# GpSimd makes the query tile with even columns first, and scores leave TensorE in natural column order

## The chip, the cores and the metric

One core of one Trainium2 chip runs the kernel. The metric is the device time of one execution in microseconds (us); a difference within 0.2% is not told from none. TensorE is PE in the profile (its weight loads PEld), VectorE is DVE, ScalarE is ACT, GpSimd is POOL, SyncE, which here only issues DMAs, is SP.

## The reference

Four batches, each with 3136 rows. A squared-ReLU attention with no softmax is followed by a feed-forward layer that has a three-tap convolution over the sequence and a sigmoid gate:

```python
scores = (1.0 / S) * np.matmul(z, z.transpose(0, 2, 1))   # S = 3136, z: (4, S, 64)
attn = np.maximum(scores, 0.0) ** 2
x = u * np.matmul(attn, v)                                # u, v: (4, S, 256)
h = np.maximum(x @ w_in, 0.0)                             # w_in: (256, 1024)
conv_out = sum(conv_w[k] * shifted(h, k - 1) for k in range(3))
out = (h * sigmoid(conv_out)) @ w_out                     # w_out: (1024, 256)
```

`z` meets itself, so the scores of a batch are a symmetric matrix.

## The kernel before

**Tiles and loops.** A batch's 3136 columns are six query blocks of 512 and a remainder of 64, and 25 key chunks of 128 (the last is half full). One pass of the main loop, a slot `k`, is one key chunk of one query block: 4 x 6 x 25 = 600 slots. In a slot PE makes the scores of a chunk four slots ahead (`scores`, two matmuls of 512 columns into the PSUM tile `s`) and adds the present chunk to the block's output (`attend`, L535). ACT takes the ReLU out of PSUM (`relu`, L490, tile `t`), DVE squares it (`square`, L504), ACT rounds the square to the high part `ah` (`split_hi`, L513), DVE subtracts to get the low part `al` (`split_lo`, a subtraction through the helper at L173). The feed-forward work of the block before is strewn between (`ffn_*`, L705 to L782). Which work stands in which slot is written out by hand: `at(slot, class, function)`; every engine takes its own instructions in that order. `manual_schedule` keeps it, and the pools only add waits.

**Two-part numbers.** Operands are `float32r` in a high and a low part: `zh`, `zl` for `z`. The rows 0 to 63 and 64 to 127 of `zh` and `zl` both hold `z`. The query tile `zq` of a block (two buffers, used in turn) holds `zh` in its lower 64 partitions and `zl` in its upper 64. Two DMAs per block, for all blocks but the first, copy it out of `zh` and `zl` (`query`, L225 and L226). The first block's is made by DVE out of the loaded `z` (`first_z`, L238 and L240). `query` for block `blk` stands eight slots ahead of the block's first slot (26 ahead for the last block of a batch).

**Reading in two streams.** `pairs` makes PE read the moving operand as columns 0, 256, 1, 257 and so on: two runs side by side. For `zq` that means that scores lie in PSUM with the two halves of the block interleaved. The consumers put it right: `split_hi` and `split_lo` read the tile through `unpair`, and so do `early_copy` (the last chunk's scores, made ahead) and the ReLU of the block's own chunks at L478. A key chunk on the diagonal reads only 256 columns, as 128 + 128.

**Reuse by symmetry.** A score tile below the diagonal isn't computed again. `part` (POOL, L434 for a whole tile; L431 and L432 for the first chunk on the diagonal) parts the ReLU tile `t` into its upper and lower 16 bits, into one of three buffers `pl`. `spill` (SP, L449) writes `pl` to DRAM, and `fetch` (SP, L457) brings it back transposed as `tp` in a later block. Where `t` came from interleaved scores (`k in mixed`), `part` also reorders: its source steps by two 4-byte numbers.

**The last chunk.** For blocks 2 to 23 the scores of chunk 24 are held as the tile `sh` and squared by DVE, which reads `sh` twice (`relu`, L482); DVE's subtraction for that chunk writes `ah` itself (64x512).

Of the kernel before, what the change touches and what calls it, by code (L numbers as in the profile page):

```python
# [8 lines left out]
F32 = mybir.dt.float32  # L9
F32R = mybir.dt.float32r  # L10
I32 = mybir.dt.int32
U16 = mybir.dt.uint16
U32 = mybir.dt.uint32
U64 = mybir.dt.uint64
AF = mybir.ActivationFunctionType
# [66 lines left out]
def kernel(  # L82
# [10 lines left out]
    nc = tc.nc  # L93
# [4 lines left out]
    P = 128  # L98
    NB = 512
# [11 lines left out]
    SC1 = 2.0**-12  # L111
# [36 lines left out]
    def at_slot(k):  # L148
        blk, i = divmod(k, NJ)
        return blk, *ent[blk // QB][blk % QB][i]  # L150
# [6 lines left out]
    zh = const.tile([P, NJ * P], F32R, name="zh")  # L157
    zl = const.tile([P, NJ * P], F32R, name="zl")
    zp = const.tile([P, P], F32R, name="zp")
# [12 lines left out]
    def sub(eng, out, a, b):  # L172
        eng.tensor_tensor(out=out, in0=a, in1=b.bitcast(F32), op=ALU.subtract)  # L173

    def copy(eng, out, a):
        (eng.copy if eng is nc.scalar else eng.tensor_copy)(out, a)  # L176


    def pairs(t):
        return t.rearrange("p (a i) -> p i a", a=2)  # L180

    def halves(t):
        return t.rearrange("p (a i) -> p a i", a=2)

    def unpair(t):
        return t.rearrange("p (i a) -> p a i", a=2)

    zst, vst, wst, wps = {}, {}, {}, {}
    LO, HI = slice(0, DQ), slice(DQ, P)
# [29 lines left out]
    zq = {}  # L219

    def query(blk):
        b, q = divmod(blk, QB)
        zq[blk] = t = mv.tile([P, NB], F32R, tag="zq", name="zq", bufs=2)
        c = slice(q * NB, (q + 1) * NB)
        nc.sync.dma_start(out=t[LO].bitcast(F32), in_=zh[LO, c].bitcast(F32))  # L225
        nc.sync.dma_start(out=t[HI].bitcast(F32), in_=zl[HI, c].bitcast(F32))  # L226

    def query_rem(b):
        zq["r"] = t = mv.tile([P, RQ], F32R, tag="zr", name="zr", bufs=1)
# [3 lines left out]
    def first_z():  # L233
        t, h = zst.pop(0), P
        v, a = nc.vector, nc.scalar
        zq[0] = x = mv.tile([P, NB], F32R, tag="zq", name="zq", bufs=2)
        copy(a, zh[:, :h], t[:, :h])
        copy(v, x, t)  # L238
        copy(a, zh[:, h:NB], t[:, h:])
        sub(v, x[HI], t[HI], x[HI])  # L240
        sub(v, zl[:, :h], t[:, :h], zh[:, :h])
        sub(v, zl[:, h:NB], t[:, h:], zh[:, h:NB])

# [104 lines left out]
    sc, ah, al, pav = {}, {}, {}, {}  # L348

    def own_cols(k):  # L350
        x = side(k)
        return slice(x * P, (x + 2) * P) if x else slice(0, NB)

    def odd(t):
        return t.rearrange("p (a b n) -> p a b n", a=2, b=2)[:, :, 1]
# [3 lines left out]
    def ring_score(blk):  # L359
        j = blk % QB * CB + CB - 1  # L360
        dg[blk] = p = ps.tile([P, 512], F32, tag="ph", name="ph", bufs=2)
        w = slice(j * P, (j + 1) * P)
        o, r = p[:, : NB // 2], odd(zq[blk]).rearrange("p a n -> p n a")
        nc.tensor.matmul(o, lhsT=zh[:, w], rhs=r, start=True, stop=False)
        nc.tensor.matmul(o, lhsT=zl[:, w], rhs=r, start=False, stop=True)

    def ring_relu(blk):
        p = dg[blk]
        dg[blk] = t = wk.tile([P, 1, 2 * NB], U16, tag="dg", name="dg", bufs=1)
        nc.scalar.activation(odd(t[:, 0].bitcast(F32)), unpair(p[:, : NB // 2]), AF.Relu, scale=SC1)  # L370

    def ring_part(blk):
        src = dg[blk][:, 0, 2 * P : 4 * P]
# [6 lines left out]
    def held(k):  # L380
        blk, j, _ = at_slot(k)
        return j == NJ - 1 and blk >= PK

    def scores(k):
        blk, j, tr = at_slot(k)
        if tr or held(k) or side(k) == CB - 1:
            return

        if k < K_O and k % 2:
            tag, n = ("ph", 2) if k < NJ else (f"o{k // 2 % 2}", 1)  # L390
        else:
            tag, n = "s", 2
        s = ps.tile([P, 512], F32, tag=tag, name="s", bufs=n)
        w, c = slice(j * P, (j + 1) * P), own_cols(k)
        r = pairs(zq[blk][:, c])
        nc.tensor.matmul(s[:, c], lhsT=zh[:, w], rhs=r, start=True, stop=False)  # L396
        nc.tensor.matmul(s[:, c], lhsT=zl[:, w], rhs=r, start=False, stop=True)  # L397
        sc[k] = s

    rl, pl, dq, dd, tp, mixed = {}, {}, {}, {}, {}, set()  # L400


    def rows_of(b, r):
# [10 lines left out]
    def part(k):  # L414
        blk, j, tr = at_slot(k)
        b, q = divmod(blk, QB)
        r, x = j // CB, side(k)
        if x is not None and x < CB - 1:
            src = rl[k][:, (x + 1) * P : (x + 2) * P if x else NB]
        elif x is None and not (tr or r < (Q0 if b == q == 0 else q + 1) or (r == QB and q >= RB)):  # L420
            src = rl[k]
        else:
            return
        n = src.shape[-1]
        pl[k] = wk.tile([P, 2, NB], U16, tag="pl", name="pl", bufs=3)[:, :, :n]
        src = src.bitcast(U16)
        if k in mixed:
            w = src.rearrange("p (i a h) -> p h a i", a=2, h=2)
            if x == 0:
                w = rl[k].bitcast(U16).rearrange("p (i a h) -> p h a i", a=2, h=2)  # L430
                nc.gpsimd.tensor_copy(pl[k][:, :, :P], w[:, :, 0, P:])  # L431
                nc.gpsimd.tensor_copy(pl[k][:, :, P:], w[:, :, 1])  # L432
            else:
                nc.gpsimd.tensor_copy(pl[k].rearrange("p h (a i) -> p h a i", a=2), w)  # L434
        else:
            nc.gpsimd.tensor_copy(pl[k], src.rearrange("p (n h) -> p h n", h=2))

    def spill(k):
        blk, j, _ = at_slot(k)
# [30 lines left out]
    def relu(k):  # L470
        x = side(k)
        if at_slot(k)[2] or x or held(k):
            if held(k):
                rl[k] = tp[k] = hs.pop(at_slot(k)[0])
            if x and x < CB - 1:
                rl[k] = tp[k]
                c = own_cols(k)
                nc.scalar.activation(halves(tp[k][:, c]), unpair(sc[k][:, c]), AF.Relu, scale=SC1)  # L478
            else:
                sc[k] = ps.tile([P, 512], F32, tag="s", name="s", bufs=2)  # L480
            if by_vector(k):
                nc.vector.scalar_tensor_tensor(  # L482
                    out=sc[k][:, :NB], in0=tp[k], scalar=SC1**-1, in1=tp[k], op0=ALU.mult, op1=ALU.mult
                )
            else:
                nc.scalar.activation(sc[k][:, :NB], tp[k], AF.Square, scale=SC1**-0.5)
            return
        mixed.add(k)
        rl[k] = wk.tile([P, NB], F32, tag="t", name="t", bufs=3)
        nc.scalar.activation(rl[k], sc[k][:, :NB], AF.Relu, scale=SC1)  # L490
        if act_squares(k):
            nc.scalar.activation(sc[k][:, :NB], rl[k], AF.Square, scale=SC1**-0.5)
# [13 lines left out]
    def split_hi(k):  # L506
        ah[k] = mv.tile([P, NB], F32R, tag="ah", name="ah", bufs=4)
        if k in tp:
            nc.scalar.activation(ah[k], tp.pop(k), AF.Square, scale=SC1**-0.5)  # L509
        elif k < DIR:  # L510
            nc.scalar.activation(ah[k], rl[k], AF.Square, scale=SC1**-0.5)
        else:
            nc.scalar.copy(halves(ah[k]), unpair(sc[k][:, :NB]))  # L513

    def split_lo(k):
        s, h = (unpair if k in mixed else halves)(sc.pop(k)[:, :NB]), halves(ah[k])
        if at_slot(k)[1] < NJ - 1:
            al[k] = mv.tile([P, NB], F32R, tag="al", name="al", bufs=3)
            sub(nc.vector, halves(al[k]), s, h)
        else:  # L520
            r = slice(HALF, P)
            sub(nc.vector, h[r], s[r], h[r])
# [20 lines left out]

    def early(blk):
        hs[blk] = p = ps.tile([P, 512], F32, tag="ph", name="ph", bufs=2)
        nc.tensor.matmul(p, lhsT=zp, rhs=pairs(zq[blk]), start=True, stop=True)

    def early_copy(blk):
        p = hs[blk]
        hs[blk] = c = wk.tile([P, NB], F32, tag="st", name="sc", bufs=4)  # L550
        nc.scalar.copy(halves(c), unpair(p))

    def early_swap(blk):
        c = hs[blk]
# [276 lines left out]
    for q in zs[2:]:  # L831
        s = min(C0.index(j) for j in range(q * CB, min(q * CB + CB, NJ))) - LA - 3
# [4 lines left out]
    for j in range(2, NJ, 2):  # L837
        i = C0.index(j)
# [5 lines left out]
    for b in range(1, B):  # L844
        k0 = (b * QB - 1) * NJ
        for q in range(QB + 1):
            s = k0 - (QB - 2 - q) * NJ + (12 if q % 2 == 0 else 4)
            if q == QB - 2:
                s = k0 + 6
            elif q == QB - 1:  # L850
                s = k0 + NJ + 6
            elif q == QB:
                s = k0 + 9
            if b == 1 and q < 2:
                s = (Q0 - QB) * NJ + NJ + k0 + 4 + 8 * q
# [3 lines left out]
        for j in range(0, NJ, 2):  # L859
            s = k0 + max(last[j] + 2, last.get(j + 1, 0) + 2, V0 + V1 * j // NJ)  # L860
            if j == NJ - 1:
                s = k0 + V0 - 2
# [5 lines left out]
    for blk in range(1, NBLK):  # L868
        s = blk * NJ + E3
# [4 lines left out]
    for blk in range(PK, NBLK):  # L874
        s = blk * NJ + (R_E if blk % QB == RB else E24[blk % QB])
# [5 lines left out]
    n = len(RN) - 1  # L881
    for b in range(B):
# [9 lines left out]
        for i in range(n + 1):  # L892
            s = k5 + (R_J + 2 * i + R_L * (i == n - 1) // 2 if i < n else R_D + 1) + 1
# [23 lines left out]
    for i, (_, what, f) in enumerate(sorted(need)):  # L917
        s = WS[i]
# [12 lines left out]
    for blk in range(NBLK - 1):  # L931
# [3 lines left out]
        for f in range(FC):  # L935
            s = k0 + FS[f]
# [119 lines left out]
    with tc.manual_schedule():  # L1056
# [8 lines left out]
        n = FC * KW  # L1065
# [95 lines left out]
```

## Time and profile before

| | |
|---|---|
| Median of 3 runs | 1512.09 us (1510.08 to 1512.25) |
| Profiled execution, whole | 1514.32 us |
| its span, first to last instruction | 1512.5 us |
| mean granted share of TensorE's clock | 0.99 |
| busy: ACT, DVE | 80%, 75% of the span |
| mean DMA rate | 140 GB/s |

The span is what the trace shows; the 1.8 us around it are start and end of the execution. Share of busy time is a mean over the span: PE is nearly always at work, so what can change are the stretches where it isn't, the rate at which it reads, and the clock that it is granted.

### The profile page before, as it was taken

The numbers are of one execution on the slowest core, as the hardware profiler recorded it, in microseconds if no ns is written. First come the engines' busy times: TensorE is split into PE (matmuls) and PEld (weight loads), VectorE is DVE, ScalarE is ACT, GpSimd is POOL, SyncE is SP. The second block draws the span as 40 slices with busy tenths as digits, with TensorE's granted clock in tenths as the row PEclk, the third lists the DMA queues.
The fourth block names the chain that finished last, engine by engine and source line by source line (L and its number), as shares of the span: only waits on it lengthen the run. The fifth ranks groups of instructions, "written<-read, shape, count | busy, mean of one in ns | idle before, by whom it ended". The sixth has DMA issues, their size and how long they took to land.

```text
span 1512.5 us, 22772 instructions
## 1 busy us (share of the span) xinstructions
PE 1467.8 (97%) x6781; PEld 1266.5 (84%) x6781; DVE 1139.8 (75%) x1714; ACT 1205.4 (80%) x2308; POOL 977.0 (65%) x1197
## 2 busy tenths in 40 slices
PE   9889999999899999999989999999998999999998
PEld 7678888888688888888878888888887888888887
DVE  8888777768777776767777777686777776777777
ACT  8878788878677888878867788877886878888777
POOL 7877666557786765645877766565596765655434
PEclk9999999999899999999999999999999999999999
DMA  6443667765445456678444556676744456477631
GB/s 190 140 143 95 162 147 162 161 149 144 130 122 154 121 152 158 144 149 177 130 132 125 149 128 146 166 157 129 176 135 121 125 136 158 114 166 158 125 73 35
DMA packets 435901, 211.01 MB, mean 140 GB/s; under 512 B 331457, under 2 KB 412609, under 8 KB 435777
## 3 DMA queue, kind: packets, MB, share of 16 engines
q1 hardware_dynamic: 435104, 209.17, 56.0%
q8 instruction: 53, 0.87, 0.2%
q14 instruction: 72, 0.58, 0.1%
q10 hardware_dynamic: 672, 0.40, 0.1%
HBM read 36.59 MB, written 86.90 MB: 82 GB/s over the span
## 4 chain that ended last, share of the span: by engine, by line
PE 64%; ACT 11%; DVE 8%; POOL 7%; issue 5%; DMA 3%; SPq 1%; ACTq 0%; POOLq 0%; DVEq 0%
PE av L535 33%; PE ph L705 4%; PE o L782 4%; PE o L780 4%; PE o L781 4%; PE ph L706 4%; PE ph L708 4%; PE s L396 3%; DVE s L482 3%; PE s L397 3%; POOL pl L434 3%; DVE ph L749 2%; PE av L617 1%; DMA dq<-pl 1%; ACT ph L744 1%
## 5 line engine op out<-in xcount | busy, mean ns | idle before, releaser
L535 PE MATMUL av<-ah,vv 128*128 128x512 f32 x2400 | 712.4, 381 | 1.7 <-ACT x L667 1.3
L173 DVE TENSOR_TENSOR al<-s,ah 128x512 fp32r<-128x512 f32 x576 | 396.8, 689 | 263.6 <-PE av L535 125.6
L535 PEld LDWEIGHTS av<-ah,vv 128*128 128x128 f32 x2400 | 451.8, 190 | 65.9 <-ACT x L667 1.7
L535 PE MATMUL av<-al,vv 128*128 128x512 f32 x1152 | 439.9, 382 | 0.7
L434 POOL COPY pl<-t 128x1024 uint16<-128x1024 uint16 x234 | 359.4, 1539 | 1.5 <-DMA dq<-pl 1.3
L173 POOL TENSOR_TENSOR gl<-hb,gh 128x512 fp32r<-128x512 f32 x192 | 250.2, 1303 | 114.0 <-ACT gh L176 113.2
L749 DVE SCALAR_TENSOR_TENSOR ph<-hb,cw,ph 128x512 f32<-128x512 f32 x384 | 286.7, 747 | 4.5 <-ACT ph L744 4.1
L504 DVE TENSOR_TENSOR s<-s,t 128x512 f32<-128x512 f32 x275 | 191.7, 697 | 77.9 <-ACT t L490 77.4
L535 PEld LDWEIGHTS av<-al,vv 128*128 128x128 f32 x1152 | 218.9, 190 | 36.0 <-DVE al L173 4.9
L513 ACT CAST ah<-s 128x512 fp32r<-128x512 f32 x277 | 163.1, 589 | 83.8 <-DVE s L504 83.4
L490 ACT ACTIVATE t<-s 128x512 f32<-128x512 f32 x277 | 165.7, 598 | 58.4 <-PE s L397 52.9
L756 ACT ACTIVATE ph<-ph 128x512 f32<-128x512 f32 (+1 forms) x200 | 115.5, 577 | 80.5 <-DVE ph L749 77.0
L509 ACT ACTIVATE ah<-tp 128x512 fp32r<-128x512 f32 x278 | 174.0, 629 | 1.9 <-PE av L535 1.7
L739 POOL COPY halo<-hb 128x2 f32<-128x2 f32 x160 | 34.0, 213 | 214.4 <-ACT hb L734 210.2
L396 PE MATMUL s<-zq,zh 128*128 128x512 f32 x323 | 123.7, 383 | 30.0 <-DVE ah L173 21.7
L705 PE MATMUL ph<-xh,wih 128*128 128x512 f32 x384 | 146.1, 380 | 1.1 <-DVE hb L763 1.1
L780 PE MATMUL o<-gh,wol 128*128 128x512 f32 x384 | 146.9, 383 | 0.0
L781 PE MATMUL o<-gh,woh 128*128 128x512 f32 x384 | 146.6, 382 | 0.0
L782 PE MATMUL o<-gl,woh 128*128 128x512 f32 x384 | 146.6, 382 | 0.0
L706 PE MATMUL ph<-xh,wil 128*128 128x512 f32 x384 | 145.5, 379 | 0.0
L763 DVE TENSOR_TENSOR hb<-ph,hb 128x512 f32<-128x512 f32 x192 | 131.8, 687 | 6.5 <-ACT ph L756 1.2
L744 ACT ACTIVATE ph<-hb,cw 128x512 f32<-128x512 f32 x192 | 133.5, 696 | 0.3
(140 smaller groups left out, 2139.1 us busy)
## 6 DMA issues: line engine op xcount, KB each, us to landing
dq<-pl SPq DMA_DIRECT2D x232, 256.0 KB, 2.7
st<-in_v_dram SPq DMA_DIRECT2D x48, 256.0 KB, 3.0
ut<-in_u_dram SPq DMA_DIRECT2D x24, 512.0 KB, 3.9
out_dram<-ob SPq DMA_DIRECT2D x19, 512.0 KB, 3.8
st<-in_z_dram SPq DMA_DIRECT2D x24, 256.0 KB, 3.1
sh<-sc SPq DMA_DIRECT2D x44, 128.0 KB, 2.4
dd<-pl SPq DMA_DIRECT2D x69, 64.0 KB, 2.1
dd<-pl SPq DMA_DIRECT2D x23, 192.0 KB, 2.5
```

Of the source, the lines that this page charges most:

```text
L173: eng.tensor_tensor(out=out, in0=a, in1=b.bitcast(F32), op=ALU.subtract)
L396: nc.tensor.matmul(s[:, c], lhsT=zh[:, w], rhs=r, start=True, stop=False)
L434: nc.gpsimd.tensor_copy(pl[k].rearrange("p h (a i) -> p h a i", a=2), w)
L504: nc.vector.tensor_tensor(out=s, in0=s, in1=rl[k], op=ALU.mult)
L509: nc.scalar.activation(ah[k], tp.pop(k), AF.Square, scale=SC1**-0.5)
L535: nc.tensor.matmul(o, lhsT=w[:, j, d], rhs=pairs(r), start=first and i == 0, stop=last and i == len(ops) - 1)
L705: nc.tensor.matmul(o, lhsT=wih[:, dc, w], rhs=pairs(xh[blk][:, dc]), start=(dc == 0), stop=False)
L706: nc.tensor.matmul(o, lhsT=wil[:, dc, w], rhs=pairs(xh[blk][:, dc]), start=False, stop=False)
L749: nc.vector.scalar_tensor_tensor(out=c, in0=hb[blk, f][:, k : e + k], scalar=cw[:, f, k : k + 1], in1=c, op0=ALU.mult, op1=ALU.add,)
L780: nc.tensor.matmul(o, lhsT=wol[:, f, d], rhs=pairs(h), start=(f == 0), stop=False)
L781: nc.tensor.matmul(o, lhsT=woh[:, f, d], rhs=pairs(h), start=False, stop=False)
L782: nc.tensor.matmul(o, lhsT=woh[:, f, d], rhs=pairs(l), start=False, stop=(f == FC - 1))
```

## The change

`query` becomes two GpSimd copies instead of two DMAs. They write each 128 columns with the 64 even columns first and the 64 odd ones behind. PE then reads a tile through `turned`: in each 128 columns, element 0, 64, 1, 65 and so on, which are the columns 0, 1, 2, 3. It is again two runs side by side, 64 elements apart instead of 256, in four pieces. Scores so lie in natural order in PSUM. All consumers of scores lose their reordering. `mixed` is gone, and `part` is one plain copy for a whole tile and one for the first chunk on the diagonal. `first_z` writes the first tile in the new order. Matmuls that don't read `zq` keep `pairs`.

```diff
+    def turned(t):
+        return t.rearrange("p (b a i) -> p b i a", a=2, i=P // 2)
+
+    def turn(t):
+        return t.rearrange("p (b i a) -> p b a i", a=2, i=P // 2)
+
+    def blocks(t):
+        return t.rearrange("p (b a i) -> p b a i", a=2, i=P // 2)
...
-        nc.sync.dma_start(out=t[LO].bitcast(F32), in_=zh[LO, c].bitcast(F32))
-        nc.sync.dma_start(out=t[HI].bitcast(F32), in_=zl[HI, c].bitcast(F32))
+        nc.gpsimd.tensor_copy(blocks(t[LO]), turn(zh[LO, c]).bitcast(F32))
+        nc.gpsimd.tensor_copy(blocks(t[HI]), turn(zl[HI, c]).bitcast(F32))
...
-        copy(v, x, t)
+        copy(v, blocks(x), turn(t))
         copy(a, zh[:, h:NB], t[:, h:])
-        sub(v, x[HI], t[HI], x[HI])
+        sub(v, blocks(x[HI]), turn(t[HI]), blocks(x[HI]))
...
-        o, r = p[:, : NB // 2], odd(zq[blk]).rearrange("p a n -> p n a")
+        o, r = p[:, : NB // 2], zq[blk].rearrange("p (c b a i) -> p c b i a", c=2, b=2, a=2)[:, :, 1]
...
-        r = pairs(zq[blk][:, c])
+        r = turned(zq[blk][:, c])
...
-        src = src.bitcast(U16)
-        if k in mixed:
-            w = src.rearrange("p (i a h) -> p h a i", a=2, h=2)
-            if x == 0:
-                w = rl[k].bitcast(U16).rearrange("p (i a h) -> p h a i", a=2, h=2)
-                nc.gpsimd.tensor_copy(pl[k][:, :, :P], w[:, :, 0, P:])
-                nc.gpsimd.tensor_copy(pl[k][:, :, P:], w[:, :, 1])
-            else:
-                nc.gpsimd.tensor_copy(pl[k].rearrange("p h (a i) -> p h a i", a=2), w)
-        else:
-            nc.gpsimd.tensor_copy(pl[k], src.rearrange("p (n h) -> p h n", h=2))
+        nc.gpsimd.tensor_copy(pl[k], src.bitcast(U16).rearrange("p (n h) -> p h n", h=2))
...
-                nc.scalar.activation(halves(tp[k][:, c]), unpair(sc[k][:, c]), AF.Relu, scale=SC1)
+                nc.scalar.activation(tp[k][:, c], sc[k][:, c], AF.Relu, scale=SC1)
...
-            nc.scalar.copy(halves(ah[k]), unpair(sc[k][:, :NB]))
+            nc.scalar.copy(ah[k], sc[k][:, :NB])
...
-        s, h = (unpair if k in mixed else halves)(sc.pop(k)[:, :NB]), halves(ah[k])
+        s, h = sc.pop(k)[:, :NB], ah[k]
...
-        nc.tensor.matmul(p, lhsT=zp, rhs=pairs(zq[blk]), start=True, stop=True)
+        nc.tensor.matmul(p, lhsT=zp, rhs=turned(zq[blk]), start=True, stop=True)
...
-        nc.scalar.copy(halves(c), unpair(p))
+        nc.scalar.copy(c, p)
```

The order of instructions moves only on POOL and SP. On SP, ahead of the second batch's first block (block 6), `query`'s two DMAs stood between the fetch of `dg` and the load of `v`, before the change:

```order
L449 DMA dd<-pl 256x1x128
L254 DMA st<-in_v_dram 128x2x256
L467 DMA_TRANSPOSE dg<-dd 128x1x256 x2
L225 DMA zq<-zh 64x512
L226 DMA zq<-zl 64x512
L254 DMA st<-in_v_dram 128x2x256
L342 DMA ut<-in_u_dram 128x2x512
```

They are gone from SP, here and in 22 other places. The copies that replace them stand on POOL. At the same place of the program POOL's rows were, before the change (`gl`: low part of the gate, `vv`: low part of `v`, `hb`, `halo`, `ends`: convolution edges):

```order
L739 COPY halo<-hb 128x2
L173 TENSOR_TENSOR gl<-hb,gh 128x512
L173 TENSOR_TENSOR vv<-st,vv 128x2x256
L724 COPY hb<-halo 128x2
L739 COPY halo<-hb 128x2
```

and with the change (its own line numbers):

```order
L737 COPY halo<-hb 128x2
L173 TENSOR_TENSOR gl<-hb,gh 128x512
L234 CAST zq<-zh 64x512
L235 CAST zq<-zl 64x512
L173 TENSOR_TENSOR vv<-st,vv 128x2x256
L722 COPY hb<-halo 128x2
L737 COPY halo<-hb 128x2
```

The two copies stand between `gl` and `vv`. POOL's next pair of such copies, for block 7, comes 57 rows later. A little later, at the first chunk on block 6's diagonal, POOL's rows were before the change:

```order
L434 COPY pl<-t 128x1024
L173 TENSOR_TENSOR gl<-hb,gh 128x512
L375 COPY pl<-dg 128x2x128
L724 COPY hb<-halo 128x2
L431 COPY pl<-t 128x2x128
L432 COPY pl<-t 128x2x256
L668 TENSOR_TENSOR ut<-x_4225,ut 128x512
```

and with the change:

```order
L435 COPY pl<-t 128x1024
L173 TENSOR_TENSOR gl<-hb,gh 128x512
L384 COPY pl<-dg 128x2x128
L722 COPY hb<-halo 128x2
L435 COPY pl<-t 128x2x384
L666 TENSOR_TENSOR ut<-x_4219,ut 128x512
```

The two pieces at L431 and L432 have become one of 384 columns; the rest stands as it did.

## Rows read from the trace of the kernel before

**Rows 1.** The page's first part: busy us (share of the span), instructions, by engine.

```profile
PE 1467.8 (97%) x6781; PEld 1266.5 (84%) x6781; DVE 1139.8 (75%) x1714; ACT 1205.4 (80%) x2308; POOL 977.0 (65%) x1197
```

**Rows 2.** Timeline, DVE, POOL, PE: start us, us, instruction, idle before it and releaser.

```profile
369.20 1.44 POOL L173 TENSOR_TENSOR xl<-ut,xh 128x512 fp32r<-128x512 f32 x1 [0.77 <-POOL vv L173]
...
398.90 7.41 DVE L482 SCALAR_TENSOR_TENSOR s<-sh 128x512 f32<-128x512 f32 x1
...
400.93 1.47 POOL L173 TENSOR_TENSOR gl<-hb,gh 128x512 fp32r<-128x512 f32 x1
...
404.46 1.29 POOL L434 COPY pl<-t 128x1024 uint16<-128x1024 uint16 x1
...
407.75 0.80 PE L396 MATMUL s<-zq,zh 128*128 128x512 f32 x1 [6.70 <-DVE ah L173]
...
415.62 0.19 POOL L739 COPY ends<-hb 128x2 f32<-128x2 f32 x1 [9.88 <-ACT hb L734]
```

**Rows 3.** Timeline of PE at the starts of the third and fourth batch.

```profile
776.55 0.79 PE L396 MATMUL s<-zq,zh 128*128 128x512 f32 x1 [6.62 <-DVE ah L173]
...
1145.60 0.79 PE L396 MATMUL s<-zq,zh 128*128 128x512 f32 x1 [6.67 <-DVE ah L173]
```

**Rows 4.** Windows, PE: stretch, us, PE busy (instructions), granted clock, DMA share, GB/s.

```profile
403.20:413.50 10.30, 5.75 (x14) 0.50 0.30 77
...
775.30:782.10 6.80, 5.55 (x13) 0.50 0.31 87
...
1143.90:1150.70 6.80, 5.10 (x12) 0.50 0.32 87
```

**Rows 5.** Windows, all engines: stretch, us; PE, PEld, DVE, ACT, POOL busy; clock, DMA.

```profile
370.50:405.80 35.30, 30.55 (x143) 26.36 (x143) 27.26 (x32) 27.06 (x51) 35.25 (x37) 0.96 0.50 153
```

**Rows 6.** POOL's groups by form: out<-in xcount, busy us, mean ns, idle before, releasers.

```profile
L434 POOL COPY pl<-t 128x1024 uint16<-128x1024 uint16 x234 | 359.4, 1539 | 1.5 <-DMA dq<-pl 1.3
L173 POOL TENSOR_TENSOR gl<-hb,gh 128x512 fp32r<-128x512 f32 x192 | 250.2, 1303 | 114.0 <-ACT gh L176 113.2 <-issue 0.2
...
L436 POOL COPY pl<-sh 128x1024 uint16<-128x1024 uint16 x18 | 20.7, 1150 | 0.0
L432 POOL COPY pl<-t 128x512 uint16<-128x512 uint16 x23 | 19.9, 865 | 0.0
...
L431 POOL COPY pl<-t 128x256 uint16<-128x256 uint16 x23 | 11.8, 512 | 0.0
...
L632 POOL COPY pl<-re 128x1024 uint16<-128x1024 uint16 x4 | 4.1, 1033 | 0.0
```

**Rows 7.** Timeline of ACT at the second batch's start: who feeds POOL's next `gl`.

```profile
398.77 0.61 ACT L176 CAST gh<-hb 128x512 fp32r<-128x512 f32 x1
```

**Rows 8.** Timeline of PE: scores of 512 columns, of 256, and the remainder's, read unpaired.

```profile
355.22 0.38 PE L396 MATMUL s<-zq,zh 128*128 128x512 f32 x1
355.43 0.38 PE L397 MATMUL s<-zq,zl 128*128 128x512 f32 x1
...
702.51 0.27 PE L396 MATMUL s<-zq,zh 128*128 128x256 f32 x1
702.62 0.28 PE L397 MATMUL s<-zq,zl 128*128 128x256 f32 x1
...
277.08 0.20 PE L592 MATMUL ph<-zr,zh 128*128 128x64 f32 x1
277.12 0.46 PE L780 MATMUL o<-gh,wol 128*128 128x512 f32 x1
277.41 0.38 PE L781 MATMUL o<-gh,woh 128*128 128x512 f32 x1
```

**Rows 9.** Timeline, DVE and POOL, ahead of block 6.

```profile
346.38 0.69 DVE L482 SCALAR_TENSOR_TENSOR s<-tp 128x512 f32<-128x512 f32 x1
...
350.97 0.19 POOL L739 COPY halo<-hb 128x2 f32<-128x2 f32 x1 [2.63 <-ACT hb L734]
```

**Rows 10.** DVE's groups by form: the copy that makes the first query tile.

```profile
L176 DVE CAST zq<-st 128x512 fp32r<-128x512 f32 x1 | 0.4, 427 | 2.1 <-DMA st<-in_z_dram 2.1
```

More of the change, by code (lines that the diff above doesn't have):

```diff
@@ L369, in ring_relu @@
         dg[blk] = t = wk.tile([P, 1, 2 * NB], U16, tag="dg", name="dg", bufs=1)
-        nc.scalar.activation(odd(t[:, 0].bitcast(F32)), unpair(p[:, : NB // 2]), AF.Relu, scale=SC1)
+        nc.scalar.activation(odd(t[:, 0].bitcast(F32)), p[:, : NB // 2].rearrange("p (b n) -> p b n", b=2), AF.Relu, scale=SC1)
     def ring_part(blk):
@@ L398, in scores @@
         sc[k] = s
-    rl, pl, dq, dd, tp, mixed = {}, {}, {}, {}, {}, set()
+    rl, pl, dq, dd, tp = {}, {}, {}, {}, {}
     def rows_of(b, r):
@@ L487, in relu @@
             return
-        mixed.add(k)
         rl[k] = wk.tile([P, NB], F32, tag="t", name="t", bufs=3)
@@ L512, in split_hi @@
         else:
-            nc.scalar.copy(halves(ah[k]), unpair(sc[k][:, :NB]))
+            nc.scalar.copy(ah[k], sc[k][:, :NB])
     def split_lo(k):
-        s, h = (unpair if k in mixed else halves)(sc.pop(k)[:, :NB]), halves(ah[k])
+        s, h = sc.pop(k)[:, :NB], ah[k]
         if at_slot(k)[1] < NJ - 1:
             al[k] = mv.tile([P, NB], F32R, tag="al", name="al", bufs=3)
-            sub(nc.vector, halves(al[k]), s, h)
+            sub(nc.vector, al[k], s, h)
         else:
```

## The prediction

> **What bounds the kernel now.** I read the page's busy shares first, then PE's waits and the timeline at the longest of them, then windows for the granted clock, then POOL's groups by form. PE is busy 1467.8 of 1512.5 us [rows 1]; with 44.7 us idle it bounds nearly every stretch, and an engine that is not PE can give back only idle time and clock. The idle time is not spread out. At the starts of the second, third and fourth batch PE stands for 6.70, 6.62 and 6.67 us at a score matmul (L396), each time until DVE's subtraction for the last chunk frees the PSUM tile `s` [rows 2, 3]: 20.0 of the 44.7 us. And each of these waits is followed, or already overlapped, by a stretch at a granted clock of 0.50, that is 1.2 instead of 2.4 GHz [rows 4].
>
> Why is DVE late there? Its squaring of `sh` (L482, both inputs in SBUF) took 7.41 us at 398.90 [rows 2], where the same operation takes about 0.69 in an undisturbed place [rows 9]. In that time POOL never paused: from 370.50 to 405.80 it was busy for 35.25 of 35.30 us [rows 5], its last pause before was 0.77 us, and its last piece ran from 404.46 to 405.75 [rows 2]. DVE's operation ended at 406.31, which is about its own duration after POOL's last piece. So I read it as follows: this form of DVE instruction does not get in while POOL reads SBUF back to back, and the length of POOL's unbroken queue is the length of the stall.
>
> The Trainium skill says the first half of this (page "SBUF — State Buffer", section "Who interferes with whom"): a VectorE instruction with two SBUF inputs contends with a GpSimd instruction that reads SBUF, and whoever issues first holds the shared ports for that instruction. The trace agrees on who blocks whom; but by the page's wording DVE would get in after one GpSimd instruction, and here it sat out the whole queue. If the Trainium skill's page were right to the letter, the 7.41 us would have another cause and the sum below would lose its first two terms (1511 instead of 1485); that is rival B.
>
> **The change, part by part.**
>
> *Parting in one run.* 234 whole-tile partings (L434) take 1539 ns in the mean; the plain parting of the same 128x1024 numbers takes 1150 (18 of them) or 1033 ns (4) [rows 6]. All whole tiles become plain: 0.39 to 0.51 us less each. I take 0.50, since the lower of the two plain rows is the one without a visible disturbance, and keep 0.39 as the bound. Over the kernel that is 91 to 118 us off POOL's 977 [rows 1]. The first chunk on the diagonal took 512 + 865 ns [rows 6]; as one run of 768 numbers it should lie under 1.0 us, 23 times 0.4 to 0.6.
>
> The Trainium skill's page "GPSIMD Engine Reference", section 7, puts a cliff in the read rate at steps of more than 8 bytes. The old parting steps by exactly 8, so by the Trainium skill it is as fast as the plain one, and the sum would be rival C's 1515 instead of 1485; the rows differ by a third at equal size, and I go by them.
>
> *The query copies.* 46 new POOL copies of 64x512, one pair for each of 23 blocks. No such copy is in the trace. From below: half of the plain parting, some 0.52 us; from above: the two-input operation on 512 numbers, 1303 ns; nearest is L432, which also moves 512 numbers with a source step of 8 bytes: 865 ns [rows 6]. I take that: 46 x 0.865 = 40 us more on POOL (24 to 60). POOL's sum so falls by about 90 us.
>
> Their latency is covered: they stand eight slots ahead, with some 2.5 us to a slot (1512.5 us for 600). What they hold is the port. Ahead of block 6 the pair comes behind a `gl`, just where DVE's squaring (L482) starts at 346.38, and POOL has 2.63 us of idle time a little later [rows 9]. So POOL absorbs the pair, but DVE may wait 1.7 us for it. What is queued behind on DVE are the subtractions that PE's next `attend` needs. I charge 1 us at each of the three batch starts, +3 (0 to 5), and nothing at the other 20 pairs, where a wait of DVE finds slack more often than not.
>
> *The three stalls.* Between the 0.77 us pause and 398.90 POOL does ten whole-tile partings. Ten times 0.39 to 0.50 puts it 3.9 to 5.0 us ahead. No query copy lies in that stretch: block 6's pair is before it and block 7's behind. POOL's `gl` in the stall was begun at 400.93 [rows 2], while its input was ready at 398.77 + 0.61 = 399.38 [rows 7]; that is a lag of 1.55 us. With a lead of 3.9 us or more POOL arrives there first and has to wait until 399.38. DVE, ready at 398.90, gets in at the latest in that gap. Its block shrinks from 6.7 to about 0.5 us. Three times: 20.0 - 1.5 = -18.5 us.
>
> *The clock.* In the three stretches at 0.50 PE was busy for 5.75, 5.55 and 5.10 us [rows 4]. At full clock that is half: -8.2 us. They begin inside the stalls, and I let them go with them.
>
> *Other waits.* 44.7 - 20.0 = 24.7 us of PE's idle time lie elsewhere, in the first block, the tail and in small waits. A POOL that is less busy shortens some of them. Estimate: -4 (0 to -10).
>
> *Nothing, or nearly so.* SP loses 46 issues and DMA 46 transfers of 128 KB; neither is on the path (the DMA mean is 140 GB/s with stretches well above). ACT and DVE read PSUM in order instead of in steps of two, at one number per step before and after; I expect no difference. In the first block DVE's copy (427 ns [rows 10]) gets a source in steps of two; at worst it takes as long as a two-input one, +0.3 us at the start, where PE waits for it.
>
> *PE's reading.* Scores of 512 columns start 0.21 us apart, and scores of 256 columns, whose two runs lie 128 apart, start 0.11 us apart [rows 8]: the same rate for runs 256 and 128 elements apart. The new reading has runs 64 apart in four pieces. From above: the remainder's 64 columns, read in one plain run, hold PE for 277.41 - 277.08 = 0.33 us together with a matmul of 512 columns, 0.09 more than 64 and 512 columns at the paired rate (0.03 + 0.21). Scaled to 512 columns this is +0.7 us. From below: no difference. The new pattern still alternates between two runs, as the paired rows do, so I take 0 and keep the other end as rival D.
>
> **The sum.** -18.5 - 8.2 - 4 + 3 + 0.3 = -27.4 us. The profiled execution had a span of 1512.5 us and 1514.3 in all; the median of the runs shown is 1512.1, within 0.2%, so the difference is taken from the median: 1484.7, say **1485**. Its own range, from the ends of the terms, is 1474 to 1494. A difference of 0.2%, 3 us, is about what can be told from none.
>
> **The rivals.**
>
> A' (0.10). The stalls shrink but don't vanish: POOL arrives early, yet its next inputs are ready so closely that DVE finds no gap at one or two of the three boundaries, and the clock falls there. What speaks for it is how narrow the gap at 399.4 is. Half of the 26.7 us stay: about 1498.
>
> B (0.04). DVE's 7.41 us has another cause than POOL's queue. Then stalls and clock stay: 1512.1 - 4 + 3.3 = 1511. Against it speaks that the block ends with POOL's queue.
>
> C (0.03). The plain parting is no faster in `t`'s place. POOL gains 40 us of work and the stalls stay: 1512.1 + 3.3 = 1515, or more if the queue at a boundary grows.
>
> D (0.07), on the other side. PE reads the four-piece pattern more slowly. 576 matmuls of 512 columns and 138 of 256 read `zq` (counted in the program), as much as 645 of 512. The forecast's gain of 27 us is used up at 27 / 645 = 0.042 us per matmul, a fifth of its time; that is the point from which the change is slower. At the plain-run price of +0.7 us it is +450 us: about 1940. For it speaks only that no row shows runs 64 apart.
>
> E (0.04). The copies are much dearer than any row suggests, or DVE waits for each pair. At 23 x 1.7 us = 39 us of stalls on PE instead of 3 the time is 1485 + 36 = 1521.
>
> The likeliest holds 0.72. It and A' are faster; B and half of E count as same; C, D and the other half of E as slower: **0.82 faster, 0.06 same, 0.12 slower**. The range reaches from the lower end of the likeliest to beyond A': **1473 to 1504**, which leaves out B to E.
>
> **What the profile after would show.** Right: L482's longest on `sh` near 1 us; no PE wait over 3 us at the starts of batches two to four and no stretch at 0.50 there; the parting group near 1.04 us; POOL's sum near 890 us; score matmuls still 0.21 us apart. If matmuls on `zq` start further apart, D is right; if the parting stays at 1.5, C; if L482 is long beside an idle POOL, B; if PE waits show up behind each query copy, E.

## The result, and the profile after

The changed kernel takes 1477.60 us (median of 4 runs, 1477.02 to 1478.06), the kernel before on the same chip 1512.15. The ratio is 0.9774, with a 95% interval of 0.9758 to 0.9791: faster by 34.5 us, 7 us more than forecast and inside the range. The profiled execution took 1477.52 us, its span is 1475.7 us.

The page's first part, for the changed kernel (the row of before is in [rows 1]):

```profile
PE 1454.0 (99%) x6781; PEld 1259.0 (85%) x6781; DVE 1119.1 (76%) x1714; ACT 1203.8 (82%) x2308; POOL 893.2 (61%) x1220
```

Between the two profiled executions the span is shorter by 36.8 us, 2.3 more than between the medians, in two parts. PE's idle time went from 44.7 to 21.7 us, which is 23.0; its busy time fell by 13.8 us, with the same number of matmuls. What became of the waits at L396 of [rows 2, 3] (now L405) is in the view of PE's waits (us in total, times, longest):

```profile
PE s L405 <- DVE al L173: 6.9, 12, 1.6
...
PE s L405 <- DVE ah L173: 0.8, 4, 0.3
```

The three waits of 6.6 to 6.7 us for `ah` are gone; the four of at most 0.3 us that are left of that kind stand at other places. The windows of PE at the starts of batches 2, 3 and 4 (stretch, us, PE busy and its instructions, granted clock, DMA share, GB/s) answer to [rows 4]:

```profile
386.00:401.00 15.00, 15.00 (x71) 1.00 0.43 128
744.00:759.00 15.00, 15.00 (x71) 1.00 0.43 129
1103.00:1118.00 15.00, 15.00 (x71) 1.00 0.43 131
```

PE does not pause and the granted clock is 1.00, that is 2.4 GHz, throughout. The timeline at the second batch's start shows where DVE's squaring of `sh` got in (compare [rows 2]), with the ACT instruction that makes the input of POOL's `gl`:

```profile
390.31 0.18 POOL L737 COPY ends<-hb 128x2 f32<-128x2 f32 x1 [1.44 <-ACT hb L732]
390.43 1.04 POOL L435 COPY pl<-t 128x1024 uint16<-128x1024 uint16 x1
391.28 0.61 ACT L176 CAST gh<-hb 128x512 fp32r<-128x512 f32 x1
391.41 0.69 DVE L481 SCALAR_TENSOR_TENSOR s<-sh 128x512 f32<-128x512 f32 x1
391.41 0.94 POOL L435 COPY pl<-tp 128x256 uint16<-128x256 uint16 x1
392.32 1.28 POOL L173 TENSOR_TENSOR gl<-hb,gh 128x512 fp32r<-128x512 f32 x1
...
395.88 1.04 POOL L435 COPY pl<-t 128x1024 uint16<-128x1024 uint16 x1
398.90 0.18 POOL L737 COPY ends<-hb 128x2 f32<-128x2 f32 x1 [1.99 <-ACT hb L732]
```

POOL had caught up and stood 1.44 us for its input. Then it ran without a pause again, until 396.92, and yet DVE took its turn, in 0.69 us, when one POOL instruction gave way to the next; it was POOL's parting of `tp` that waited (0.94 us; in the third batch's stall of before it took 0.39).

POOL's groups by form (count, busy us, mean ns) answer to [rows 6]:

```profile
L173 POOL TENSOR_TENSOR gl<-hb,gh 128x512 fp32r<-128x512 f32 x192 | 249.4, 1299 | 144.9 <-ACT gh L176 141.8 <-PE s L406 2.4 <-DMA dq<-pl 0.6
L435 POOL COPY pl<-t 128x1024 uint16<-128x1024 uint16 x234 | 242.5, 1038 | 1.6 <-ACT ah L511 0.5 <-DMA dq<-pl 0.2
...
L234 POOL CAST zq<-zh 64x512 fp32r<-64x512 f32 x23 | 20.7, 898 | 0.0
...
L235 POOL CAST zq<-zl 64x512 fp32r<-64x512 f32 x23 | 20.2, 877 | 1.4
L435 POOL COPY pl<-t 128x768 uint16<-128x768 uint16 x23 | 18.9, 822 | 0.7 <-DMA dq<-pl 0.7
```

The parting fell from 1539 to 1038 ns, and POOL's idle time ahead of `gl`, waiting for ACT's `gh`, rose from 114.0 to 144.9 us: POOL is early now. Scores on the new `zq` still follow each other at the old pace (timeline of PE, answering to [rows 8]):

```profile
421.71 0.38 PE L405 MATMUL s<-zq,zh 128*128 128x512 f32 x1
421.92 0.38 PE L406 MATMUL s<-zq,zl 128*128 128x512 f32 x1
422.14 0.38 PE L778 MATMUL o<-gh,wol 128*128 128x512 f32 x1
```

### The profile page after: what moved, and what is told of

Same layout as the page of the kernel before. It is cut to its first block, busy times and chain, and to the rows that moved or that the text cites. A ratio compares the mean times of both kernels' runs of the same rounds, so it can differ in the third digit from the quotient of the medians.

```text
span 1475.7 us, 22865 instructions
## 1 busy us (share of the span) xinstructions
PE 1454.0 (99%) x6781; PEld 1259.0 (85%) x6781; DVE 1119.1 (76%) x1714; ACT 1203.8 (82%) x2308; POOL 893.2 (61%) x1220
## 4 chain that ended last, share of the span: by engine, by line
PE 80%; ACT 9%; DVE 5%; issue 3%; POOL 2%; DMA 1%; SPq 0%; ACTq 0%; POOLq 0%; DVEq 0%
PE av L533 41%; PE ph L703 5%; PE o L780 5%; PE o L778 5%; PE ph L704 5%; PE o L779 5%; PE ph L706 5%; PE s L405 4%; PE s L406 4%; DVE ph L747 2%; PE av L615 2%; DVE s L481 1%; ACT ph L742 1%; ACT hb L732 1%; ACT t L488 1%
## 5 line engine op out<-in xcount | busy, mean ns | idle before, releaser
L173 POOL TENSOR_TENSOR gl<-hb,gh 128x512 fp32r<-128x512 f32 x192 | 249.4, 1299 | 144.9 <-ACT gh L176 141.8
L435 POOL COPY pl<-t 128x1024 uint16<-128x1024 uint16 (+1 forms) x257 | 261.4, 1019 | 2.4 <-DMA dq<-pl 0.9
L405 PE MATMUL s<-zq,zh 128*128 128x512 f32 x323 | 121.1, 375 | 7.8 <-DVE al L173 6.9
```

Source lines behind the costliest of these rows:

```text
L435: nc.gpsimd.tensor_copy(pl[k], src.bitcast(U16).rearrange("p (n h) -> p h n", h=2))
```

## The experiments

All ratios are to the kernel before on the same chip, with 95% intervals.

**Which part of the change gains.** Four kernels, run together. The first makes only the query copies, in natural order; the second only the plain partings:

```diff
-        nc.sync.dma_start(out=t[LO].bitcast(F32), in_=zh[LO, c].bitcast(F32))
-        nc.sync.dma_start(out=t[HI].bitcast(F32), in_=zl[HI, c].bitcast(F32))
+        nc.gpsimd.tensor_copy(t[LO], zh[LO, c].bitcast(F32))
+        nc.gpsimd.tensor_copy(t[HI], zl[HI, c].bitcast(F32))
```

> The kernel before, with the query tile made by two plain GpSimd copies (columns in their order) instead of two DMAs; partings and reading as before. Theory T (the gain comes from GpSimd's faster parting, which keeps VectorE's squaring of sh from being shut out): the three waits of 6.6 to 6.7 us at the starts of batches 2 to 4 stay, with their stretches at a granted clock of 0.50, and POOL's sum rises by about 41 us to 1018; 1512 to 1520 us. Rival R1 (the gain comes from taking the 46 transfers off SP and the DMA queues): most of the 34.5 us, 1478 to 1490. Rival R2 (it comes from ScalarE and VectorE reading scores in natural order): 1512 as well.

Measured: 1514.79 us, ratio 1.0020 (1.0011 to 1.0029). The three waits stayed, the longest 6.7 us, and a squaring of `sh` that was short before was shut out too (timeline of DVE):

```profile
469.19 3.93 DVE L482 SCALAR_TENSOR_TENSOR s<-sh 128x512 f32<-128x512 f32 x1
```

So taking the transfers away gains nothing; the kernel with the copies takes 2.6 us longer.

```diff
-        if k in mixed:
-            w = src.rearrange("p (i a h) -> p h a i", a=2, h=2)
...
-        else:
-            nc.gpsimd.tensor_copy(pl[k], src.rearrange("p (n h) -> p h n", h=2))
+        nc.gpsimd.tensor_copy(pl[k], src.rearrange("p (n h) -> p h n", h=2))
```

> The kernel before, with every parting as one plain run, and the query tile still by two DMAs, scores still interleaved in PSUM. Left out: the reordering of the parted tiles, so the columns of reused scores are in another order. Theory T: the three waits and the stretches at 0.50 are gone, POOL's sum is about 893 - 41 = 852 us; 1473 to 1479 us, the changed kernel's 1477.6 less what its query copies cost (0 to 4). R1 (transfers): 1505 to 1515. R2 (natural order for ScalarE and VectorE): 1505 to 1515, since their reading is as before.

Measured: 1475.51 us, ratio 0.9760 (0.9744 to 0.9776): all of the gain and 2.1 us more, with the query by DMA and the scores still interleaved in PSUM. (As it leaves out the reordering, it could not replace the changed kernel.) PE's waits:

```profile
PE s L396 <- DVE al L173: 5.3, 11, 1.6
...
PE s L396 <- DVE ah L173: 1.1, 4, 0.3
```

The third takes the stalled instruction from DVE and leaves POOL as slow as it was:

```diff
-        return k // NJ % QB >= DS and k % 2 == 1 or held(k)
+        return k // NJ % QB >= DS and k % 2 == 1 and not held(k)
```

> The kernel before, with the square of the held last chunk (sh) on ScalarE, which the two-input squaring of VectorE is replaced by; everything else as before, the slow partings too. Theory T: what stalls is the VectorE instruction with two SBUF inputs beside GpSimd's unbroken queue; with none there the three waits of 6.6 to 6.7 us shrink to under 2 and the stretches at 0.50 go with them: 1480 to 1492 us, though POOL is as slow as before. Rival B (the 7.41 us have another cause, sh or what follows is late anyway): the waits stay at 5 us or more, 1508 to 1514.

Measured: 1487.21 us, ratio 0.9831 (0.9816 to 0.9845). No wait at L396 was longer than 2.1 us and the mean granted clock was 1.000. It was DVE's squaring, then, and not `sh` itself. The fourth puts the stepped parting back into the changed kernel, the rest as changed:

```diff
+        if side(k) is None and k not in tp and n == NB:
+            w = src.bitcast(U16).rearrange("p (i a h) -> p h a i", a=2, h=2)
+            nc.gpsimd.tensor_copy(pl[k].rearrange("p h (a i) -> p h a i", a=2), w)
+        else:
+            nc.gpsimd.tensor_copy(pl[k], src.bitcast(U16).rearrange("p (n h) -> p h n", h=2))
```

> The changed kernel, with the whole-tile partings read again in steps of two 4-byte numbers. Wrong on account of it: the column order of the reused scores. Theory T: POOL's parting is back at about 1.54 us, its sum at about 1005 us, and the three waits with their stretches at 0.50 are back: 1510 to 1520 us. R1 and R2 (transfers, natural order): within 5 us of the changed kernel, 1478 to 1483.

Measured: 1515.61 us, ratio 1.0020 (1.0011 to 1.0029). The stall is back where it was (timeline of DVE, POOL and PE at the third batch's start):

```profile
769.37 7.45 DVE L485 SCALAR_TENSOR_TENSOR s<-sh 128x512 f32<-128x512 f32 x1
...
769.73 1.58 POOL L437 COPY pl<-t 128x1024 uint16<-128x1024 uint16 x1
...
775.18 1.07 POOL L437 COPY pl<-t 128x1024 uint16<-128x1024 uint16 x1
...
778.26 0.79 PE L405 MATMUL s<-zq,zh 128*128 128x512 f32 x1 [6.74 <-DVE ah L173]
```

All four came out as the prediction's reading said (GpSimd's queue keeps DVE's squaring out), and the two rival sources of the gain (fewer transfers, natural order for ACT and DVE) fell.

**Around the change.** What a plain reading of `zq` would cost PE, and three places for work that moved. For the first, `zq` also comes by the two DMAs again, in natural column order; the cut shows only the reading:

```diff
     def turned(t):
-        return t.rearrange("p (b a i) -> p b i a", a=2, i=P // 2)
+        return t
```

> The changed kernel, with the query tile by two DMAs in natural column order and read by TensorE in one plain run of 512 columns; scores are in natural order in PSUM as in the changed kernel, partings plain. It prices the two-run reading. By the remainder's plain 64 columns (0.09 us dearer) scaled to 512: 0.9 us from one score matmul to the next, some 1900 us. If those 0.09 us belong to the narrow shape and plain reading is as fast: 0.21 us apart, 1474 to 1479 us.

Measured: 1483.62 us in a single execution. The timeline of PE, at the place that was shown of the changed kernel:

```profile
421.65 0.40 PE L405 MATMUL s<-zq,zh 128*128 128x512 f32 x1
421.88 0.39 PE L406 MATMUL s<-zq,zl 128*128 128x512 f32 x1
422.11 0.38 PE L778 MATMUL o<-gh,wol 128*128 128x512 f32 x1
```

Neither expectation held. Plain scores of 512 columns are 0.23 us apart, where two runs give 0.215. PE was busy for 8.7 us more than in the kernel with plain partings and the same DMAs (1463.2 against 1454.5). The prediction's upper bound of 0.7 us for each matmul was some 40 times too high: it scaled up what a matmul of 64 columns had cost beyond its share.

The held square on ScalarE, in the changed kernel (the edit is that of the third kernel above):

> The changed kernel, with the square of the held last chunk (sh) on ScalarE instead of VectorE. Theory T: the stall that this cures in the kernel before is gone already, so there is nothing left to cure: within 2 us of 1477.6. Rival: part of the stall still hides in the changed kernel's waits at the batch starts, 1472 to 1475.

Measured: 1482.09 us, ratio 0.9813 (0.9781 to 0.9845), outside both expectations: 4.5 us more than the changed kernel took on its chip. No gain hid there; moving the square has a cost of its own. The query copies on other engines:

```diff
-        nc.gpsimd.tensor_copy(blocks(t[LO]), turn(zh[LO, c]).bitcast(F32))
-        nc.gpsimd.tensor_copy(blocks(t[HI]), turn(zl[HI, c]).bitcast(F32))
+        copy(nc.vector, blocks(t[LO]), turn(zh[LO, c]).bitcast(F32))
+        copy(nc.vector, blocks(t[HI]), turn(zl[HI, c]).bitcast(F32))
```

> The changed kernel, with the query copies on VectorE instead of GpSimd: about 0.43 us each by the first tile's copy, 20 us in all on an engine that is idle for a quarter of the span. If the copies cost what they cost on account of GpSimd's ports and queue (theory T: the 2 us by which the kernel with plain partings and DMAs for the query is faster), 1475 to 1477; if what costs is VectorE waiting, 1478 to 1482.

Measured: 1489.60 us, ratio 0.9863 (0.9831 to 0.9894), above both expectations; a copy took 0.73 to 0.82 us there in the mean, not 0.43. With `nc.scalar` in place of `nc.vector`:

> The changed kernel, with the query copies on ScalarE instead of GpSimd: about 0.6 us each by ScalarE's cast of 512 columns, 28 us in all on an engine that is idle for 18% of the span. If they find slack, 1475 to 1478; ScalarE's ReLU is the first step behind each score, so each pair may hold TensorE up by 0 to 1 us: up to 1500.

Measured: 1484.41 us, ratio 0.9830 (0.9792 to 0.9868), inside the second expectation; 0.87 us for a copy. Both engines work on every score behind PE, and both are the worse place. POOL, the engine with the most idle time, is the right one; none of these beats the changed kernel, nor does any other here that keeps the columns of reused scores in order.

**What shuts VectorE out.** In the changed kernel DVE got in beside a POOL that had just begun a new unbroken queue, so "an unbroken queue" could not be all. In every stall a tiny copy (`ends`) follows within the squaring's first quarter of a microsecond. The next kernel takes it away, another makes POOL later:

```diff
-        nc.gpsimd.tensor_copy(halo[:, f] if q < QB - 1 else ends[:, f, b], t[:, NB : NB + 2])
+        if q < QB - 1:
+            nc.gpsimd.tensor_copy(halo[:, f], t[:, NB : NB + 2])
+        else:
+            nc.scalar.copy(ends[:, f, b], t[:, NB : NB + 2])
```

> The kernel before, with the 32 tiny copies that keep a batch's last two columns (ends<-hb, 128x2, 0.18 us) on ScalarE instead of GpSimd. In all three stalls such a copy stands right behind the low part of v, within 0.24 us of the start of VectorE's squaring; in the changed kernel the squaring got in within 0.69 us although POOL's queue was unbroken there from 390.31 to 396.92 us. Theory U (what the prediction said: an unbroken queue of POOL shuts VectorE out until it ends): POOL's queue is 0.1 us shorter, the stalls stay at 6.5 us or more; 1510 to 1514 us. Theory H (VectorE gets its turn when one POOL instruction gives way to the next, but misses it where the next is such a tiny copy just as VectorE starts, and then misses all that follow): no tiny copy, no stall; the squaring takes 1.4 us at most, 1482 to 1492 us.

Measured: 1509.33 us, ratio 0.9967 (0.9941 to 0.9992). The stalls stayed, without any tiny copy near (timeline of DVE):

```profile
396.07 6.57 DVE L482 SCALAR_TENSOR_TENSOR s<-sh 128x512 f32<-128x512 f32 x1
```

Theory H, which blamed the tiny copy, fell.

```diff
+        if q == QB - 1 and f == 2:
+            for _ in range(4):
+                nc.gpsimd.tensor_copy(spare, t[:, :2])
```

> The kernel before, with four more tiny GpSimd copies (128x2, to a spare tile) in each batch, some 8 us ahead of the batch's end, inside POOL's unbroken queue: POOL has more to do and arrives 0.4 to 0.5 us later at the place of the stall, with its queue still unbroken. Theory U: the stalls stay and grow by 0 to 0.5 us each; 1512 to 1516 us. Theory H: the handover from the low part of v to the tiny copy now falls 0.5 to 0.7 us behind the start of the squaring instead of 0.07 to 0.24, and VectorE takes that turn as it does everywhere else; stalls and stretches at 0.50 are gone although GpSimd is busier, 1482 to 1492 us.

Measured: 1489.65 us, ratio 0.9833 (0.9786 to 0.9881). GpSimd had more to do, and the three stalls were gone. Timeline of POOL and DVE ahead of the second batch, and a later row:

```profile
387.63 1.01 POOL L742 COPY spare<-hb 128x2 f32<-128x2 f32 x4
...
395.68 1.29 POOL L174 TENSOR_TENSOR vv<-st,vv 128x512 fp32r<-128x512 f32 x1
...
396.43 1.11 DVE L483 SCALAR_TENSOR_TENSOR s<-sh 128x512 f32<-128x512 f32 x1
396.92 0.66 POOL L743 COPY ends<-hb 128x2 f32<-128x2 f32 x1
...
458.91 3.93 DVE L483 SCALAR_TENSOR_TENSOR s<-sh 128x512 f32<-128x512 f32 x1
```

Theory U, the prediction's own wording, fell with this as well: POOL had no less work queued. But the four copies, which wrote one tile, had waited for each other, 0.25 us apart: by the records POOL had paused three times for 0.06 us, 8 us ahead of the squaring. And at another place, the end of a batch's first block, two squarings took 3.93 us in this kernel, behind three POOL instructions (2.1 us) that followed each other without a pause. The last two kernels give every copy a place of its own:

```diff
+        if q == QB - 1 and f == 2:
+            for i in range(4):
+                nc.gpsimd.tensor_copy(spare[:, i], t[:, :2])
```

> As the kernel with four more tiny GpSimd copies in each batch, but each to a place of its own, so that none waits for the one before it. There the four took 1.01 us where they stood, 0.25 apart, with pauses of about 0.1 us between them, and VectorE got in at the next batch end. Here they should stand 0.12 us apart, without pauses: POOL is 0.48 us later than in the kernel before, its queue of 28 us unbroken. Theory P (what decides is whether POOL has paused at all, however briefly, in the microseconds ahead: behind a long unbroken queue VectorE loses the first handover and then all others): the three stalls stay, 6.8 to 7.9 us; 1512 to 1517 us. Theory A (what decides is at which moment of a POOL instruction VectorE asks, so that any shift helps): the stalls are gone, 1482 to 1492 us.

Measured: 1510.67 us, ratio 0.9995 (0.9968 to 1.0022), with all three stalls (7.43, 7.43, 7.58 us). Timeline at the same place:

```profile
387.80 0.59 POOL L742 COPY spare<-hb 128x2 f32<-128x2 f32 x4
...
396.29 7.43 DVE L483 SCALAR_TENSOR_TENSOR s<-sh 128x512 f32<-128x512 f32 x1
```

> As the one with four tiny copies in places of their own, with eight: POOL is 0.96 us later than in the kernel before, its queue unbroken. Theory P: the stalls stay, 7.3 to 8.4 us; 1513 to 1519 us. Theory A: gone, 1482 to 1492 us, or at the least different from the kernel with four.

Measured: 1505.82 us, ratio 0.9974 (0.9951 to 0.9997). DVE missed the first turn in all three places, but in two of them it got in two turns later:

```profile
396.87 1.27 POOL L174 TENSOR_TENSOR vv<-st,vv 128x512 fp32r<-128x512 f32 x1
...
397.62 2.70 DVE L483 SCALAR_TENSOR_TENSOR s<-sh 128x512 f32<-128x512 f32 x1
...
1123.98 7.58 DVE L483 SCALAR_TENSOR_TENSOR s<-sh 128x512 f32<-128x512 f32 x1
```

Theory P held for the first turn, not for all that follow. Theory A fell in its strong form: with POOL some 1 us later, as in the kernel whose copies paused, the stalls were not gone. The same two kernels settle it more sharply. In both the squaring begins 0.73 to 0.82 us after POOL's `vv` (396.43 and 395.68 there, 397.62 and 396.87 here), so DVE asks at the same moment of the same POOL instruction; it got in at the first change in three of three with the pauses and in none of three without. A's weaker form, that eight copies differ from four, came out, so that the moment may bear on the later turns.

Counted over the traces of the fourteen kernels, one execution each, where a squaring of this form (two inputs in SBUF) met a POOL instruction with at least 0.1 us to run and the next right behind it: behind queues of up to nine instructions without a pause it ended 0.55 to 0.58 us after the running one, that is in the first turn, in 549 of 554 cases; six that began together with the POOL instruction and went ahead of it are left out. Behind queues of 27 to 37 instructions, which had run for some 30 us, it missed the first turn in 18 of 18; 16 of these stayed out until POOL paused, 2 got in at the third turn.

Executions differ, and only one of each kernel was traced. The 54 of the kernel before that were timed with these experiments range from 1502 to 1521 us; the three shortest show a mean granted clock of 0.994 or 0.995, the four longest of 0.988 to 0.990, most of the others 0.991 to 0.993. Whether all three stalls come in every execution was therefore not seen.

## Why the prediction was right

**The three stalls: right, size -18.5, measured -20.0.** The 20.0 us [rows 2, 3] are gone altogether: at the three batch starts PE is busy for 15.00 of 15.00 us, where the prediction left a wait of 0.5 us each. That faster parting alone does this is shown from both sides: by the kernel with nothing else, and by the changed kernel with the old parting.

**How VectorE gets in: the step that was wrong, and its outcome partly luck.** The prediction said that DVE "does not get in while POOL reads SBUF back to back" and would enter "at the latest in that gap", where POOL has to wait for the input of `gl`. There was no such gap. The input was ready at 391.28 + 0.61 = 391.89, and POOL began `gl` at 392.32 right behind its parting of `tp`; it did not pause before 396.92. DVE asked at 391.41. Had it needed a gap, these rows would have kept it out for some 5.5 us, against 7.41 for the whole squaring before, and most of each stall would have stayed. It entered at a change of POOL's instructions instead, as it commonly does. What the runs show is narrower than the prediction's reading: behind a queue that has run for some 30 us DVE misses its turn, and three pauses of 0.06 us, 8 us earlier, restore it. POOL's lead brought such a pause (1.44 us at 390.31), so the lead did matter, but not in the way that was written. The Trainium skill (page "SBUF — State Buffer", section "Who interferes with whom") has the ports held for one instruction, which the prediction set against the stall; in 549 of 554 cases behind short queues the trace agrees with the page, and in the 18 behind long ones it does not.

**The clock: -8.2, right for the three stretches.** The profiled execution of the kernel before has a fourth stretch at half clock, in the first batch, behind one more stall: DVE's L305, an integer operation in SBUF, took 3.28 us beside POOL, and PE waited 3.18. Timeline and window of the kernel before, then the window of the changed kernel:

```profile
92.84 3.28 DVE L305 TENSOR_SCALAR wr<-wr 128x256 uint32<-128x256 uint32 x1
...
96.98 0.80 PE L396 MATMUL s<-zq,zh 128*128 128x512 f32 x1 [3.18 <-DVE al L173]
```

```profile
96.00:103.00 7.00, 6.02 (x15) 0.51 0.34 103
```

```profile
96.00:103.00 7.00, 7.00 (x34) 1.00 0.59 166
```

15 matmuls in those 7 us before, 34 now. At 0.51 of the clock the 6.02 us are some 3.0 more than at full clock; the wait, now at most 1.6 us, gives another 1.5. But this stall is no fixed cost of the kernel before. Five other kernels have the same program up to this point (the one with the held square on ScalarE, and the last four above), and in none of their traces does it stand here. The longest DVE operation and wait of the five, with the held square on ScalarE:

```profile
93.77 1.64 DVE L305 TENSOR_SCALAR wr<-wr 128x256 uint32<-128x256 uint32 x1
...
96.80 0.48 PE L396 MATMUL s<-zq,zh 128*128 128x512 f32 x1 [2.07 <-DVE al L173]
```

In all five the clock from 96 to 103 us was 1.00; two of them (the kernel with `ends` on ScalarE and the one whose copies paused) had one at half clock near 60 us instead. The profiled execution also has a mean granted clock of 0.990, most others of this kernel 0.991 to 0.993. So these 4.5 us belong to the 36.8 us between the two profiles; how much of them is in the 34.5 between the medians is not known.

**Other waits: -4, mis-sized.** By the medians, the kernel with partings alone gains 36.6 us; less 20.0 and 8.2 this leaves 8.4 us for everything else, where the term had -4 (0 to -10). This is the largest part, 4.4, of the 7.1 us by which the gain was under-sized; the stalls are 1.5 of it and the terms for the query copies and the first block 1.2. Between the profiles, PE's busy time fell by 13.8 us, of which the four stretches explain 11.2; the other 2.6 us were not traced.

**The query copies: +3, measured 2.1 to 2.6,** by the kernel without them and the kernel with them alone, which is little more than can be told from none. Their durations, 898 and 877 ns, are close to the 865 taken. They do not hold DVE up where the prediction charged it: at 338.89, ahead of block 6, the squaring took 0.69 us and the copy behind it had to wait (1.36 us):

```profile
338.89 0.69 DVE L481 SCALAR_TENSOR_TENSOR s<-tp 128x512 f32<-128x512 f32 x1
338.91 1.36 POOL L234 CAST zq<-zh 64x512 fp32r<-64x512 f32 x1
```

**The parting: right.** It takes 0.50 us less for each of 234, and 0.82 us in all for the first chunk on the diagonal, where the two pieces took 512 + 865 ns. POOL's sum fell by 84 us, not 90.

**PE's reading and natural order: right at nothing.** Two runs 64 apart are read as fast as two runs 256 apart. ACT's copy that makes `ah` out of PSUM took 591 ns in the mean, before 589; DVE's subtraction for `al` 689, before 689. DVE's first copy took 428 ns for 427, so the 0.3 charged was nothing.

Of the rivals, A' did not occur (no boundary kept a long wait), B fell with the held square on ScalarE, C by the row of 1038 ns, D by the spacing of the scores; E's mechanism, a wait of DVE for each pair, did not show at the pair ahead of block 6, and the price of all pairs, 2.1 to 2.6 us, leaves no room for it. The prediction's own range, 1474 to 1494, is somewhat wider than the ends of its terms, which give 1475 to 1491.

## What to carry to other kernels

When an engine that is "only 65% busy" runs without a pause for tens of microseconds ahead of a stall, look at whom it keeps out of SBUF before looking at its busy share: here 28 of the 34.5 us that an edit to GpSimd gained appeared in TensorE's waits and clock, through one VectorE instruction at the start of each batch but the first. Test such a reading from three sides, as here: the suspected part alone, the suspected part undone, and the victim moved to another engine. Make GpSimd read SBUF in one run where another engine can put the order right for nothing, and look for a stall in the traces of several executions before sizing the gain: the three at the batch starts came again, the one in the first batch did not.

## What the runs showed of the hardware that was not expected

- Turns between VectorE and GpSimd: the counts above, 549 of 554 against 0 of 18. Why a long queue makes VectorE miss its turn stays open. A tiny copy beside the start (the stalls stayed at 6.57 us without it) and the moment of asking (the first change of instructions, 0.07 to 1.01 us behind the squaring's start, was missed every time) are excluded; that GpSimd's next instructions have then long had their inputs fits, but was not tried. No queue of between 9 and 27 instructions was met. A long queue is not needed either: the five exceptions behind short queues, three of them 3.93 us long, all stand at one place, the end of the first block of a batch, where the same alignment at other times let VectorE in.
- The stepped parting was slow beside working engines and not beside standing ones: in the kernel with the old parting put back it took 1.58 us at 769.73, beside TensorE and ScalarE, and 1.07 at 775.18, when both had stood for some 4 us; the plain one takes 1.04 beside a busy TensorE. This is read from rows, not from an experiment, and which of the two engines matters is not shown.
- TensorE reads 512 columns in one plain run in 0.23 us, in two runs side by side in 0.215, whether these lie 256 or 64 apart; 256 columns whose runs lie 128 apart take 0.11 [rows 8].
